# Zero fills of a scratch buffer in an attention and expert kernel: 640 rows an expert from 80 partitions in place of 608 rows from 76

## The chip, the core and the metric

One core of one Trainium2 chip runs the whole program. The metric is the device time of one execution in microseconds (us), lower is better.

## What is computed

Thresholded attention over 4 batches, 8 heads, 576 positions, head size 64; then a layer of 8 experts in which each of the 2304 tokens goes to one expert; then a gated product with two wide matrices. Cut to what matters:

```python
scores = scale * q @ k.T
scores = where(scores >= max(scores) - tau, scores, -1e9)
attn   = softmax(scores)
x      = (attn @ v) as 2304 rows of 512
e      = argmax(x @ w_gate)             # one of 8 experts for each row
x[row] = gate[row] * (relu(x[row] @ w1[e]) @ w2[e])
out    = (x @ w_a) * (x @ w_b) @ w_out
```

## The kernel before, in words

Attention runs head pair by head pair: 16 iterations (4 batches of 4 pairs), each of 9 tiles of scores. For one iteration SyncE (SP) issues the loads of q, k and v (`load`, lines 373, 379 and 381). GpSimd (POOL) splits each into a high and a low part (`split_units`, lines 400 and 414; `raw_k` gives `sk`, `raw_q` gives `sq`, `rv` gives `sv`). TensorE (PE) transposes them (`tq`, line 440), ScalarE (ACT) and VectorE (DVE) write `kT` and `qT`, and SP copies half of `kT` to the other 64 partitions (`swap`, line 446, a transfer of 64 partitions inside the on-chip memory). PE makes the scores (`S_J`, `S_A`, `S_B`, line 654), DVE and ACT the maxima and exponentials, PE transposes the result (line 762), ACT and POOL split it (lines 712 to 727, 803 and 804), SP moves one piece of it across partitions (`tk<-half`, line 783, 64 partitions again), and PE multiplies by v (`pv`, line 838).

After every fourth iteration the rows of a batch are scattered into the scratch buffer `xs` in device memory (helper `scatter`, line 44): one region of 2304 rows for each expert, filled from its start. Later the expert with most rows is read as its first `LEAD` = 256 rows, and the experts as eight items of up to 352 rows, at most 256 rows on. A region can hold fewer tokens than are read, so its first rows are set to zero before the first scatter: 8 experts in `FILLS` = 4 pieces each, 32 transfers (`zero_fill`, line 390). Their source is a tile of zeros in on-chip memory that is read twice by each partition:

```python
n = self.zero_rows // FILLS
self.nc.sync.dma_start(
    self.xs[lo:lo + n].rearrange("(p r) d -> p r d", r=2),
    self.z[0:n // 2].unsqueeze(1).to_broadcast([n // 2, 2, DM]))
```

The order of all work in the attention stage is written out by hand in the string `ORDER` (words `z:0` to `z:31` are the fills, `qe:i:sk0` and `qe:i:sk2` the swaps, `k:i:0` and `k:i:1` the `tk` moves); the fills stand in the first six of the 16 iterations, one to four in a row, between loads, swaps and `tk` moves on SP, which issues them in that order. All of them share one queue, q1. The tile of zeros has the buffer of the scaled rows `xg` of the first batch (tag `xg`, line 1788), so the first write of `xg` (ACT, line 1018) comes after the last fill.

After attention come the experts (from about 420 us) and the gated product (from about 760 us), in which PE multiplies with weights loaded by SP.

Of the kernel before, what the change touches and what calls it, by code (L numbers as in the profile page):

```python
# [31 lines left out]
LEAD = 256  # L32

FILLS = 4
# [1723 lines left out]
@with_exitstack  # L1758
def attention_experts_gated(ctx, tc, q, k, v, tau, w_gate, w1, w2, wa, wb, wo, out):
    nc = tc.nc  # L1760
    NT = q.shape[0] * S
    c = ctx.enter_context(tc.tile_pool(name="consts", bufs=1))
    dp = ctx.enter_context(tc.tile_pool(name="scratch", bufs=1, space=DRAM))
    xs = dp.tile([E * NT, DM], F32, name="xs")
    idt = dp.tile([NT, 1], I32, name="idt")
    idf = c.tile([P, P], F32, name="idf")
    make_identity(nc, idf)
    idr = c.tile([P, P], F32R, name="idr")
    nc.vector.tensor_copy(idr, idf)
    consts = dict(idf=idf, idr=idr)  # L1770
    nb = NT // S
    routing = dict(
        oh=c.tile([P, NB * nb, E], BF16, name="oh"),
        slot=c.tile([P, NB * nb], F32, name="slot"),
        base=c.tile([P, E], F32, name="base"),
        scatters=[],
        lead_relu=[None, None, None],
        lead_high=None,
        sel=c.tile([P, E], F32, name="sel"),
        kept=c.tile([P, 1], F32, name="kept"),  # L1780
        lead=c.tile([P, 1], I32, name="lead"),
        y=[dp.tile([P, 4, LEAD], F32, name=f"lead_y{r}") for r in range(2)],
    )
    routing.update(Experts.constants(nc, c, NT))
    with ExitStack() as ac:
        att = Attention(ac, tc, q, k, v, tau, w_gate, w1, w2, xs, routing, consts)

        att.z = att.xp.tile([P, 4, H, D], F32, tag="xg", name="zero")[:, 0].rearrange("p h d -> p (h d)")
        att.zero_rows = LEAD + max(n for _, n in Experts.ITEMS)
        nc.vector.memset(att.z, 0.0)  # L1790
        att.run()
    ex = Experts(ctx, tc, xs, w1, w2, wa, wb, wo, out, routing, consts, NT)
    ex.order()
    ex.chunk_count()
    ex.experts(idt)
    ex.gated(idt)
# [29 lines left out]
```

## Time and profile before

| what | us |
|---|---|
| median of three runs (1099.53 to 1104.93) | 1100.19 |
| the profiled execution, its own time | 1100.29 |
| its span, first to last instruction | 1098.6 |
| PE busy | 1011.1 (92%) |
| DVE busy | 716.3 (65%) |
| ACT busy | 542.8 (49%) |
| POOL busy | 560.8 (51%) |

Busy time is a sum over a span of stages with different limits; what a stage is limited by is read from the stage's own stretch. A stretch of the trace can be asked for the busy time of each engine, for the granted TensorE clock (1.00 is full), and for the share of 16 DMA engines that were moving packets. A row of the timeline gives the start, the duration, the instruction, and in brackets how long the engine had been idle before and what ended that.

### The profile page before, as it was taken

Reading aid. Unit: us, or ns where it says so; the run is one execution under the profiler, and the core shown is the slowest. Engines: PE = TensorE matmul, PEld = TensorE weight load, DVE = VectorE, ACT = ScalarE, POOL = GpSimd, SP = SyncE. Lnnn points to the kernel's source line nnn. Section 1 sums busy time; section 2 is a strip of 40 time slices with the busy share of each in tenths; the row PEclk is TensorE's granted clock in tenths of the full one; section 3 lists DMA queues with packets and bytes.
Section 4 is the critical chain, followed back from the end, with each engine's and each line's share of the span. In section 5 each row is a group of like instructions: output and inputs, shape, how many; then the busy total and the mean of one; then the engine's idle time right before and its main releaser. Section 6 shows DMA issues by size and latency. Waiting matters only on the chain.

```text
span 1098.6 us, 18663 instructions
## 1 busy us (share of the span) xinstructions
PE 1011.1 (92%) x6392; PEld 918.0 (84%) x6392; DVE 716.3 (65%) x1472; ACT 542.8 (49%) x1118; POOL 560.8 (51%) x515
## 2 busy tenths in 40 slices
PE   3577696999998989999999999999999999999996
PEld 3476696999998989999999998888888888888885
DVE  5655595999999974545568957974592773953213
ACT  4555585999998853545555535321231221321110
POOL 4535566899998764111113426662462653623234
PEclk9978898999999999999999999999999999999999
DMA  5445454545434447665566612340030130200012
GB/s 147 117 125 140 133 134 149 134 114 140 124 78 134 128 137 242 215 193 174 181 188 205 203 48 78 60 75 20 20 78 20 43 73 1 77 20 1 20 58 96
DMA packets 111106, 118.68 MB, mean 108 GB/s; under 512 B 19648, under 2 KB 82112, under 8 KB 111008
## 3 DMA queue, kind: packets, MB, share of 16 engines
q1 hardware_dynamic: 106766, 106.66, 35.0%
q0 software_dynamic: 3840, 10.50, 2.5%
q8 instruction: 51, 0.84, 0.3%
q14 instruction: 47, 0.39, 0.1%
q10 hardware_dynamic: 402, 0.29, 0.1%
HBM read 77.57 MB, written 20.46 MB: 89 GB/s over the span
## 4 chain that ended last, share of the span: by engine, by line
PE 68%; DVE 7%; issue 6%; DMA 6%; POOL 5%; ACT 4%; SPq 3%; POOLq 0%; DVEq 0%; ACTq 0%
PE pg L1709 21%; PE po L1735 10%; PE ph_i L1521 9%; PE py_i L1542 8%; PE pv L838 5%; PE tp L762 3%; PE S_A L654 2%; DMA kT<-kT 2%; PE S_B L654 2%; DMA tk<-half 2%; PE tx L864 2%; PE S_J L654 1%; POOL out L44 1%; SPq L390 1%; DVE mt L667 1%
## 5 line engine op out<-in xcount | busy, mean ns | idle before, releaser
L1709 PE MATMUL pg<-y,w 128*128 128x512 f32 (+1 forms) x1440 | 301.9, 368 | 0.0
L1709 PEld LDWEIGHTS pg<-y,w 128*128 128x128 f32 x1440 | 251.6, 189 | 45.3
L1735 PE MATMUL po<-w,g 128*128 128x512 f32 x648 | 153.3, 390 | 0.6 <-DVE acc L1740 0.6
L1722 POOL TENSOR_TENSOR g<-gg,g 128x512 fp32r<-128x512 f32 (+1 forms) x58 | 76.2, 1313 | 151.1 <-ACT g L1720 151.0
L1735 PEld LDWEIGHTS po<-w,g 128*128 128x128 f32 x648 | 121.0, 188 | 26.1 <-issue 0.8
L727 POOL TENSOR_TENSOR pt<-st,pt 128x512 fp32r<-128x512 f32 x93 | 118.8, 1284 | 18.4 <-ACT pt L717 15.1
L1413 POOL TENSOR_TENSOR w<-raw,w 128x512 fp32r<-128x512 f32 x33 | 45.2, 1372 | 152.1 <-ACT w L1412 152.0
L1521 PE MATMUL ph_i<-xt_i,w 128*128 128x256 f32 (+4 forms) x768 | 117.0, 298 | 3.2 <-DVE w L1413 2.4
L1720 ACT CAST g<-gg 128x512 fp32r<-128x512 f32 (+1 forms) x60 | 34.7, 578 | 169.2 <-PE po L1735 96.2
L1718 DVE TENSOR_TENSOR gg<-ga,pg 128x512 f32<-128x512 f32 (+1 forms) x60 | 37.7, 628 | 122.4 <-PE pg L1709 122.4
L1542 PE MATMUL py_i<-h_i,w 128*128 128x256 f32 (+4 forms) x768 | 112.5, 294 | 0.3 <-PEq L1636 0.3
L838 PE MATMUL pv<-pt,sv 128*128 128x288 f32 x512 | 107.4, 328 | 4.9 <-POOL pt L727 3.6
L1521 PEld LDWEIGHTS ph_i<-xt_i,w 128*128 128x128 f32 x768 | 104.7, 189 | 5.4 <-DVE w L1413 3.6
L1542 PEld LDWEIGHTS py_i<-h_i,w 128*128 128x128 f32 x768 | 104.9, 189 | 0.7 <-issue 0.6
L762 PE MATMUL tp<-idf,P 128*128 128x128 f32 x504 | 94.8, 281 | 3.5 <-DVE P L687 1.6
L1740 DVE TENSOR_TENSOR acc<-acc,po 128x512 f32<-128x512 f32 x108 | 72.7, 683 | 34.3 <-PE po L1735 34.2
L1443 POOL TENSOR_TENSOR t<-t,w 128x512 f32<-128x512 f32 x36 | 53.2, 1477 | 64.0 <-ACT w L1442 47.8
L838 PEld LDWEIGHTS pv<-pt,sv 128*128 128x128 f32 x512 | 77.9, 197 | 6.2 <-POOL pt L727 3.8
L1412 ACT CAST w<-raw 128x512 fp32r<-128x512 f32 x128 | 75.8, 620 | 14.5 <-DMA raw<-in_moe_w 6.9
L1413 DVE TENSOR_TENSOR w<-raw,w 128x512 fp32r<-128x512 f32 x95 | 68.3, 730 | 12.5 <-ACT w L1412 10.6
L762 PEld LDWEIGHTS tp<-idf,P 128*128 128x128 f32 x504 | 64.9, 145 | 5.6 <-DVE P L687 1.9
L1716 ACT COPY ga<-pg 128x512 f32<-128x512 f32 (+1 forms) x60 | 32.6, 544 | 68.6 <-PE pg L1709 68.6
(245 smaller groups left out, 1889.3 us busy)
## 6 DMA issues: line engine op xcount, KB each, us to landing
raw<-in_moe_w SPq DMA_DIRECT2D x128, 256.0 KB
xs<-zero SPq DMA_DIRECT2D x32, 304.0 KB
tk<-half SPq DMA_DIRECT2D x64, 144.0 KB
raw<-in_moe_w_a SPq DMA_DIRECT2D x12, 512.0 KB
raw<-in_moe_w_b SPq DMA_DIRECT2D x12, 512.0 KB
raw<-in_moe_w_out SPq DMA_DIRECT2D x12, 512.0 KB
kT<-kT SPq DMA_DIRECT2D x32, 160.0 KB
kT<-kT SPq DMA_DIRECT2D x32, 144.0 KB
```

Source lines behind the costliest of these rows:

```text
L654: nc.tensor.matmul(ps[:, n, 0:HALF], lhs, kT[:, r, k0 + n * HALF:k0 + (n + 1) * HALF], start=(j == 0), stop=(j == len(seq) - 1),)
L727: nc.gpsimd.tensor_sub(lo, st, fr(hi))
L762: nc.tensor.transpose(st["ps"][:, 128 * j:128 * j + 128], parts(j), idf)
L838: nc.tensor.matmul(R["v", n][:, 0:HALF], lhs, z, start=(c == 0 and r == 0), stop=(c == 4))
L1412: nc.scalar.copy(hi_t, raw)
L1413: engine.tensor_sub(lo_t, raw, fr(hi_t))
L1521: nc.tensor.matmul(ps[:, 0:n], w[a][:, k, :], xt[b][k][:, 0:n], start=(s_ == 0), stop=(s_ == len(steps) - 1))
L1542: nc.tensor.matmul(st["y"][d][:, 0:n], w[a][:, 0, d * P:d * P + P], h[b][:, 0:n], start=(f == 0 and d % each == 0 and (a, b) == (0, 0)), s ...
L1709: mm = nc.tensor.matmul(ps[:, 0:n], w[g][j][m][a][:, k, :], self.y[b][:, k, c0:c0 + n], start=(s_ == 0), stop=(s_ == len(steps) - 1))
L1722: last = low.tensor_sub(gl[:, 0:n], gt[:, 0:n], fr(gh)[:, 0:n])
L1735: nc.tensor.matmul(ps, res[j][a][:, t * P:t * P + P], w[g][j][2][b][:, 0, :], start=(s_ == 0), stop=(s_ == len(steps) - 1))
L1740: nc.vector.tensor_tensor(acc[:, tt, :], acc[:, tt, :], ps, op=ALU.add)
```

## The change

The rows an expert are rounded up to a multiple of 32 times `FILLS`, so that a piece is 160 rows from 80 partitions in place of 152 rows from 76:

```diff
-        att.zero_rows = LEAD + max(n for _, n in Experts.ITEMS)
+        att.zero_rows = -(-(LEAD + max(n for _, n in Experts.ITEMS)) // (32 * FILLS)) * 32 * FILLS
```

The 32 transfers stand at the same places of the same queue, each of 320 KB in place of 304 KB; every engine has the same instructions in the same order as before. No other transfer changes.

## Rows read from the trace of the kernel before

**Rows 1.** The page's 40 equal slices of the span (27.5 us each), busy tenths and clock.

```profile
PE   3577696999998989999999999999999999999996
...
PEclk9978898999999999999999999999999999999999
```

**Rows 2.** The fills' instructions on SP: duration in ns least, median, most; first and last start.

```profile
L390 SPq DMA_DIRECT2D xs<-zero x32: 684/744/4216, 17.9 to 170.4; - x32
```

**Rows 3.** Busy time by stretch: us, engines, clock, DMA share of 16 engines, GB/s.

```profile
20.00:40.00 20.00, 14.02 (x97) 12.10 (x96) 17.32 (x39) 15.63 (x30) 12.27 (x13) 1.00 0.42 124
40.00:190.00 150.00, 104.89 (x736) 100.29 (x736) 87.98 (x220) 89.94 (x190) 83.60 (x85) 0.84 0.50 135
190.00:350.00 160.00, 156.25 (x1268) 149.33 (x1266) 150.05 (x378) 150.46 (x321) 145.35 (x147) 1.00 0.43 116
```

**Rows 4.** Waits of PE from 40 to 190 us: in total, times, longest.

```profile
PE pv L838 <- DMA tk<-half: 26.7, 4, 10.9
PE S_J L654 <- DMA kT<-kT: 9.2, 2, 6.2
PE pv L838 <- POOL pt L727: 3.6, 1, 3.6
PE S_B L654 <- DVE P L687: 3.3, 2, 3.1
PE pv L838 <- POOL pt L804: 0.8, 1, 0.8
```

**Rows 5.** Timeline of SP, issues of loads among the fills and after them.

```profile
33.67 1.61 SPq L373 DMA_DIRECT2D raw_k<-in_k  x1
...
36.87 4.00 SPq L373 DMA_DIRECT2D raw_q<-in_q  x1
...
207.68 0.47 SPq L373 DMA_DIRECT2D raw_q<-in_q  x1
```

**Rows 6.** Timeline of POOL, splits that wait for loads.

```profile
46.63 0.67 POOL L400 TENSOR_SCALAR sk<-raw_k 128x576 fp32r<-128x576 f32 x1 [7.26 <-DMA raw_k<-in_k]
...
168.44 0.72 POOL L400 TENSOR_SCALAR sv<-rv 128x640 fp32r<-128x640 f32 x1 [6.87 <-DMA rv<-in_v]
```

**Rows 7.** Timeline of ACT, the first write of `xg`.

```profile
181.87 0.72 ACT L1018 ACTIVATE xg<-x,g 128x512 f32<-128x512 f32 x1 [3.07 <-DMA xs<-zero]
```

**Rows 8.** Timeline of DVE, what waited for ACT's next exponential.

```profile
183.25 0.82 DVE L687 SCALAR_TENSOR_TENSOR P<-S_B,m_B,e_B 128x576 f32<-128x576 f32 x1 [3.11 <-ACT e_B L675]
```

**Rows 9.** Waits of PE from 190 to 350 us.

```profile
PE pv L838 <- DMA tk<-half: 0.4, 1, 0.4
```

**Rows 10.** DMA from 168 to 176 us: packets by size; the queue's packets, MB, share of 16 engines.

```profile
DMA packets 374, 0.74 MB, mean 93 GB/s; under 512 B 13, under 2 KB 13, under 8 KB 374
...
q1 hardware_dynamic: 374, 0.74, 26.0%
```

**Rows 11.** DMA from 17.9 to 176 us, from the first fill on: the same queue.

```profile
q1 hardware_dynamic: 15249, 20.40, 47.3%
```

**Rows 12.** DMA from 176 to 178 us, when swaps of `kT` are under way: the queue.

```profile
q1 hardware_dynamic: 195, 0.39, 84.8%
```

**Rows 13.** Timeline of PE, score products after a wait and without one.

```profile
133.81 1.78 PE L654 MATMUL S_J<-kT,qj 128*128 128x288 f32 x6 [6.25 <-DMA kT<-kT]
...
205.67 1.30 PE L654 MATMUL S_J<-kT,qj 128*128 128x288 f32 x8
```

**Rows 14.** DMA from 1060 to 1098.6 us, when `out` is written: GB/s in 40 slices, the queue.

```profile
GB/s 127 144 17 259 13 0 0 0 0 0 0 8 0 0 98 174 272 170 102 0 272 0 0 0 0 0 246 106 191 225 144 174 0 272 191 81 0 8 0 0
...
q0 software_dynamic: 970, 3.15, 21.4%
```

## The prediction

> **What bounds the kernel now.** First the page's slices [rows 1]: from the eighth slice on (about 190 us) PE is busy nine tenths nearly throughout, but before that it stands between 3 and 7 tenths in all slices but one, and the granted clock dips below full in most of them. The kernel is bound by PE except in its first 190 us, and the 32 fills are issued from 17.9 to 170.4 us [rows 2], inside that part.
>
> Second, the stretches [rows 3]. From 190 to 350 us the same attention work runs with no fill: 1268 matmuls in 160 us, PE idle for 3.75 us, clock 1.00. From 40 to 190 us only 736 matmuls are done in 150 us: PE is idle for 150 − 104.89 = 45.1 us and the mean clock is 0.84. At the later pace (160 / 1268 = 0.1262 us a matmul) 736 take 92.9 us, so this stretch loses **57.1 us**. DVE, ACT and POOL are no busier there than 60%, so none of them is the limit. From 20 to 40 us PE also has gaps, but I leave that stretch out: it is the first iteration, with DVE busy 17.3 of 20 us.
>
> Third, what ends PE's waits from 40 to 190 us [rows 4]. DMA ends 26.7 us (`tk`) and 9.2 us (`kT`) directly. 3.6 us come through POOL: its split of `raw_k` started at 46.6 us after a wait of 7.3 us for a load issued at 33.7 us, 13 us earlier [rows 5, 6]. 0.8 us comes through POOL's wait of 6.9 us for `rv` [rows 6]. And 3.1 of the 3.3 us behind DVE come from the first write of `xg`, in whose buffer the zeros lie: ACT waited 3.07 us there for the fills, its next exponential was late, and DVE waited 3.11 us for that [rows 7, 8]. Together 26.7 + 9.2 + 3.6 + 0.8 + 3.1 = **43.4 us** of the 45.1 us end in a transfer. From 190 to 350 us PE waits 0.4 us for `tk` and for no other DMA [rows 9]: the moves are the same, the fills are gone.
>
> Fourth, why the transfers are late. From 168 to 176 us the queue moves almost nothing but fills: 361 of 374 packets are 2 KB or more, and the share is 26.0% of 16 engines, which is 4.2 engines, at 93 GB/s [rows 10]. I read this as a fill from 76 partitions lying on **four of the 16 DMA engines**. A packet then takes 0.26 x 16 x 8 us / 374 = 89 ns. One fill is 152 rows of 2 KB: 13.5 us of engine time, 3.4 us on four engines. 32 fills are 433 us, or 108 us on each of the four. All of the queue from 17.9 to 176 us is 47.3% of 16 engines for 158.1 us, 1197 us [rows 11]. The 764 us that are not fills, spread evenly, make 48 us on each engine. So four engines have 108 + 48 = 156 us of work in 158 us and are full, and the other twelve have 48. A transfer spread over all engines lands when its slowest part does, so each `kT`, `tk` and load waits behind the fills on those four. The queue also pushes back on SP: issuing a `raw_q` load took 4.00 us at 36.9 us and 0.47 us at 207.7 us [rows 5].
>
> **The change part by part.**
>
> *More bytes.* 8 more rows a fill, 32 times: 256 packets of 89 ns, 23 us of engine time, 1.4 us on each of 16 engines. SP issues the same 32 transfers at a median of 744 ns [rows 2] in the same order. Cost on the path: nothing, as long as the engines aren't full; if they stayed on four, 23 / 4 = 5.7 us.
>
> *Spread.* No row shows 80 partitions. The nearest are the swaps, of 64: from 176 to 178 us, right after the fills drained, swaps of `kT` alone hold 84.8% of 16 engines, that is 13.6 or more [rows 12]. So it isn't a small number of partitions that confines a transfer; 64 divides evenly among 16 engines and 76 doesn't, and 80 does, by five each. Bounds: four engines as now (no gain) and 16. I take 16, as nearest to the swaps. A fill is then 160 x 89 / 16 = 0.89 us on each engine in place of 3.4 us on four, against 0.74 us to issue it: a run of four fills leaves well under a microsecond of backlog in place of some ten. Work for each engine: 32 x 0.89 + 48 = 76 us, where four had 156.
>
> The Trainium skill ("DMA: Bandwidth & Descriptors", Why a DMA increments its semaphore by 16 and not by 1) says that a transfer gets the largest number up to 16 that divides the slowest dimension on both sides, which makes 4 of 76 and 16 of 80; no row shows the second. The same page (Specifications) gives 8 partitions an engine as a convention, which would put 76 and 80 both on ten engines and leave the time where it is; the 26.0% above, 4.2 engines rather than ten, speak against it.
>
> *Waits that go.* The 43.4 us above, if each transfer lands as it does after 190 us. *The clock.* After each long wait PE runs at the lower of its two levels for a while: six `S_J` products took 1.78 us after a wait of 6.25 us, and eight took 1.30 us with no wait [rows 13]. Over the stretch 736 matmuls took 104.89 us where the later mean (156.25 / 1268 = 123 ns) makes 90.7 us: 14.2 us more, and these go with the waits. Sum: 43.4 + 14.2 = 57.6 us, the same as the 57.1 us from the pace, which I take as the ceiling since the later stretch is bound by PE.
>
> *What is late next.* Not all of it comes back. The 764 us of other traffic and the fills' 456 us must now fit in some 110 us of 16 engines, a share near 0.7, where the undisturbed stretch has 0.43 [rows 3]. `tk` is the one move that was late there at all [rows 9], so it has no slack, and behind a run of fills it will be late again by one or two microseconds. Six or so such places with a short dip of the clock: I leave **10 us** in, an estimate between 0 and half of the 57. After 190 us PE is busy throughout, so what comes earlier there brings the end forward by as much.
>
> Gain: 57 − 10 = 47 us. The profiled execution took 1100.29 us, a span of 1098.6 and 1.7 around it, 0.1 us from the median of the runs: 1100.3 − 47 = **1053 us**.
>
> **The rivals.**
>
> *A half gain.* The fills, now on all 16 engines in runs of up to four, still hold up every `tk` and swap behind them, and PE falls back to the lower clock each time. For it: the share of 0.7. Against: nothing was late at 0.43, and the fills drain about as fast as SP issues them. A third to a half of the 57 us comes back: 1072 to 1081 us.
>
> *Nothing changes.* The fills stay on few engines, or the four full engines weren't what the moves waited for. For it: no row shows 80 partitions. Against: the four-engine share stands at 26% while the swaps reach 85%. Time 1100 us, at most 1106 with the added bytes.
>
> *Slower, by the far end of the fills.* If 93 GB/s [rows 10] is what device memory takes in from this pattern rather than what four engines give, a fill of 320 KB holds all 16 queues for 3.5 us in place of four. Other transfers end with their slowest part, so they gain nothing, and the fills' added 5% (0.18 us each) come on top: 32 x 0.18 = 5.7 us, 1106 us. It decides from the point at which a fill takes over 3.4 us to drain. Against: at the end the writes of `out`, into the same memory, reach 272 GB/s in a slice, and 3.15 MB take 21.4% of 16 engines for 38.6 us, 24 GB/s an engine [rows 14], the same as 93 / 4 = 23. The rate follows the engines.
>
> **How the numbers follow.** A measurement of this kernel tells a difference of about 0.5% (5.5 us) from none. The forecast, 35 to 59 us faster, has 0.76; a half or third of the gain 0.17; nothing 0.04; slower 0.03. So faster 0.93, same 0.04, slower 0.03. The low end is the whole 57 us and two for what 20 to 40 us may give: 1041. The high end takes in most of the half gain, 20 us: 1080. What lies outside is the weaker end of the half gain and the two last cases, near 0.15.
>
> **What would show it.** Right: no stretch with a DMA share flat near 0.26 before 190 us; a fill's packets draining near 0.9 us; raw loads issued in about half a microsecond; PE's waits for `tk` and `kT` down from 36 us to under 10, the clock near 1.00 from 50 us on; the matmuls that ended at 190 us now ending near 143 us, and every later stage as long as before. Wrong: fills still at 26% (the spread); spread fills but `tk` waits of several microseconds each (the 10 us); or a gain before 190 us that is given back in the experts' weights.

## The result, and the profile after

| | us |
|---|---|
| before, median of four runs (1099.53 to 1104.93) | 1100.36 |
| changed, median of four runs (1043.88 to 1050.26) | 1049.39 |
| changed, the profiled execution, its own time | 1050.08 |
| its span | 1048.4 |

The ratio is 0.9518, with a 95% interval of 0.9476 to 0.956: 51 us faster, 4 us more than forecast and inside the range.

The page's slices after (26.2 us each), against [rows 1]:

```profile
PE   3899999999989899999999999999999999999996
...
PEclk9999999999989999999999999999999999999999
DMA  5877645436343486655666223510220310300012
```

From the third slice on PE is at nine tenths, but for two slices at eight; it used to be there from the eighth slice on. The busy time by stretch, with the columns of [rows 3]:

```profile
20.00:40.00 20.00, 14.04 (x95) 12.13 (x95) 17.12 (x39) 15.37 (x30) 12.67 (x14) 1.00 0.72 199
40.00:143.00 103.00, 100.94 (x815) 96.74 (x815) 96.34 (x243) 97.58 (x208) 89.55 (x92) 1.00 0.70 196
143.00:190.00 47.00, 45.37 (x365) 43.12 (x364) 42.12 (x103) 42.65 (x92) 43.29 (x44) 1.00 0.44 120
190.00:350.00 160.00, 154.22 (x1218) 147.65 (x1216) 145.03 (x364) 140.44 (x296) 134.89 (x136) 0.98 0.44 121
```

The stretch in which the fills lie now runs at the pace of the stretch without them: 103 / 815 = 0.1264 us a matmul, against 0.1262 after 190 us before the change. The clock is 1.00 in it, and the DMA share is 0.70, as worked out. From 20 to 40 us PE's busy time did not change.

All waits of PE from 40 to 143 us that the view lists, where five rows of up to 26.7 us stood [rows 4]:

```profile
PE tp L762 <- ACT pt L717: 0.5, 1, 0.5
PE tp L762 <- ACT qT L458: 0.4, 1, 0.4
PE S_B L654 <- DVE P L687: 0.4, 2, 0.3
PE tp L762 <- DVE x L872: 0.4, 1, 0.4
PE pv L838 <- ACT o L843: 0.2, 1, 0.2
```

No DMA is among them. The fills' instructions on SP [rows 2], and a `raw_q` load issued behind three fills [rows 5], after:

```profile
L390 SPq DMA_DIRECT2D xs<-zero x32: 605/628/1814, 18.1 to 119.0; - x32
```

```profile
33.83 0.49 SPq L373 DMA_DIRECT2D raw_q<-in_q  x1
```

The queue pushes back far less: 0.49 us for the issue that took 4.00 us, though the `raw_k` load just ahead of it still took 1.23 us (1.61 before).

On how many engines a fill from 80 partitions lies is read from 118 to 123 us, while the last four fills drain. SP issued them from 116.87 to 120.22 us:

```profile
116.87 3.35 SPq L390 DMA_DIRECT2D xs<-zero  x4
```

```profile
DMA packets 715, 1.33 MB, mean 267 GB/s; under 512 B 70, under 2 KB 70, under 8 KB 714
...
q1 hardware_dynamic: 714, 1.32, 93.2%
```

93.2% is 14.9 engines, so these fills lie on all 16. A packet takes 0.932 x 16 x 5 / 714 = 104 ns, a little more than the 89 ns before. 320 KB at 267 GB/s are 1.2 us a fill, and the fills drain until about 123 us (from 123 to 124 us the share is 9.9%), nearly 3 us after the last was issued.

**Where the gain ends up.** Taking the same instruction in both traces shows how far it has moved. Two issues of SP before, in order of time, and the same two after:

```profile
206.66 0.37 SPq L373 DMA_DIRECT2D raw_k<-in_k  x1
...
950.96 0.37 SPq L1432 DMA_DIRECT2D raw<-in_moe_w_b  x1
```

```profile
150.26 0.37 SPq L373 DMA_DIRECT2D raw_k<-in_k  x1
...
900.76 0.37 SPq L1432 DMA_DIRECT2D raw<-in_moe_w_b  x1
```

Right behind the fills the program is 206.66 − 150.26 = 56.4 us ahead, in the gated product (whose first product, L1709, starts at 644 us before, not at about 760) only 950.96 − 900.76 = 50.2 us. So between these two executions 6.2 us were given back on the way, in places that have no fill. Two of them show in PE's timeline, before:

```profile
351.49 1.11 PE L864 MATMUL tx<-W,o 128*128 128x72 f32 x8 [2.64 <-DVE half L721]
...
627.09 1.46 PE L1521 MATMUL ph_i<-xt_i,w 128*128 128x256 f32 x10 [1.92 <-DVE w L1413]
```

and after, the same products behind the same waits:

```profile
296.31 1.99 PE L864 MATMUL tx<-W,o 128*128 128x72 f32 x8 [2.65 <-DVE half L721]
...
575.37 2.31 PE L1521 MATMUL ph_i<-xt_i,w 128*128 128x256 f32 x10 [1.92 <-DVE w L1413]
```

PE waited equally long in both kernels. Before, it came back at the higher of its two levels (the granted clock was 1.00 from 351 to 355 us), after, at the lower one (0.50 from 296 to 300 us). Whether this belongs to the change is asked in the last run.

### The profile page after: what moved, and what is told of

It reads as the page before. It is cut to its first block, busy times and chain, and to the rows that moved or that the text cites. A ratio compares the mean times of both kernels' runs of the same rounds, so it can differ in the third digit from the quotient of the medians.

```text
span 1048.4 us, 18663 instructions
## 1 busy us (share of the span) xinstructions
PE 1002.2 (96%) x6392; PEld 909.6 (87%) x6392; DVE 715.5 (68%) x1472; ACT 541.0 (52%) x1118; POOL 560.8 (53%) x515
## 4 chain that ended last, share of the span: by engine, by line
PE 51%; issue 5%; POOL 3%; DVE 3%; ACT 1%; DMA 0%; POOLq 0%; SPq 0%; DVEq 0%; ACTq 0%
PE pg L1709 22%; PE po L1735 10%; PE ph_i L1521 9%; PE py_i L1542 9%; POOL out L44 1%; PE px_i L1496 1%; POOL w L1444 1%; POOL t L1443 1%; DVE w L1413 1%; DVE acc L1740 1%; DVE a L1435 1%; POOL g L1722 0%; DMA raw<-in_moe_w 0%; DVE t L1439 0%; DVE u L1436 0%
## 5 line engine op out<-in xcount | busy, mean ns | idle before, releaser
L1709 PE MATMUL pg<-y,w 128*128 128x512 f32 (+1 forms) x1440 | 301.9, 368 | 0.0
L1709 PEld LDWEIGHTS pg<-y,w 128*128 128x128 f32 x1440 | 251.6, 188 | 45.3
L1735 PEld LDWEIGHTS po<-w,g 128*128 128x128 f32 x648 | 120.9, 188 | 26.2 <-issue 0.8
L838 PE MATMUL pv<-pt,sv 128*128 128x288 f32 x512 | 103.3, 320 | 0.2 <-ACT o L843 0.2
L762 PE MATMUL tp<-idf,P 128*128 128x128 f32 x504 | 91.9, 274 | 3.7 <-DVE P L687 1.6
L838 PEld LDWEIGHTS pv<-pt,sv 128*128 128x128 f32 x512 | 74.9, 190 | 0.9 <-ACT o L843 0.5
L1526 DVE SCALAR_TENSOR_TENSOR h_i<-ph_i,h_i 128x256 fp32r<-128x256 f32 (+4 forms) x64 | 28.9, 451 | 60.5 <-ACT h_i L1525 60.5
L1525 ACT ACTIVATE h_i<-ph_i 128x256 fp32r<-128x256 f32 (+4 forms) x64 | 26.0, 407 | 84.4 <-PE ph_i L1521 63.7
```

The costliest lines, as they stand in the source:

```text
L762: nc.tensor.transpose(st["ps"][:, 128 * j:128 * j + 128], parts(j), idf)
L838: nc.tensor.matmul(R["v", n][:, 0:HALF], lhs, z, start=(c == 0 and r == 0), stop=(c == 4))
L1709: mm = nc.tensor.matmul(ps[:, 0:n], w[g][j][m][a][:, k, :], self.y[b][:, k, c0:c0 + n], start=(s_ == 0), stop=(s_ == len(steps) - 1))
L1735: nc.tensor.matmul(ps, res[j][a][:, t * P:t * P + P], w[g][j][2][b][:, 0, :], start=(s_ == 0), stop=(s_ == len(steps) - 1))
```

## The experiments

The theory to be tested: a fill lies on a number of DMA engines that its partitions set, the full engines make every other transfer late, and it is the spread alone, not the 32 rows more, that gave the 51 us. The rivals: the round number of rows; a fixed number of partitions for an engine; a queue's order in place of full engines. Each run has the kernel before beside it on the same chip, with medians of 1099.8 to 1100.5 us. The 106 us that the expectations name is the changed kernel's stretch from 18 to 124 us, the counterpart of 17.9 to 176 us before [rows 11].

### 608 rows, all spread

```diff
-        n = self.zero_rows // FILLS
-        lo = e * self.NT + part * n
+        n = (160, 160, 160, 128)[part]
+        lo = e * self.NT + part * 160
```

> 608 rows an expert as before, but in pieces of 160, 160, 160 and 128 rows from 80, 80, 80 and 64 partitions. Theory (a transfer lies on the largest number of engines up to 16 that divides its partitions evenly, and four engines were full): all pieces lie on 16 engines, each engine has 433 / 16 + 48 = 75 us of work, so the time is that of the change, 1047 to 1051 us, and no stretch shows a DMA share near 0.26. Rival (the number of rows matters, 640 being a round number): 608 rows stay at 1100 us.

Measured: 1048.17 us, ratio 0.9534 (0.9507 to 0.9561), the time of the change. Of the two things that the change does, rows and partitions, only the partitions count. The rival is out.

### 77 partitions

```diff
+        att.zero_rows = 154 * FILLS
```

> 616 rows an expert, 154 from 77 partitions. Theory: 77 divides evenly by 11, so 11 engines with 32 x 154 x 0.089 / 11 + 48 = 88 us of work, below the 106 us that the first part takes in the changed kernel: 1047 to 1055 us. Rival (rows, or that only a multiple of 16 partitions helps): near 1100 us.

Measured: 1048.61 us, ratio 0.9543 (0.9516 to 0.9569). One partition more than before, and the whole gain is there. Where fills run nearly alone (119.5 to 122 us) the queue shows

```profile
q1 hardware_dynamic: 243, 0.45, 61.2%
```

which is 9.8 of the eleven engines of the theory. It need not be 16. An issue of a fill took SP 910 ns here (the median), where the change has 628, and that cost nothing.

### 85 partitions

```diff
+        att.zero_rows = 170 * FILLS
```

> 680 rows an expert, 170 from 85 partitions: more rows and more partitions than the change. Theory: 85 divides evenly by 5, so five engines with 32 x 170 x 0.089 / 5 + 48 = 145 us of work, 39 us over the 106 us of the changed kernel's first part: about 1088 us (1078 to 1098), and a DMA share near 5 / 16 = 0.31 where the fills run alone. Rivals (rows; or eight partitions to an engine, which gives 85 partitions 11 engines): 1050 to 1054 us.

Measured: 1102.85 us, ratio 1.0027 (1.001 to 1.0043). More partitions than in the change, and none of the gain, which puts both rivals out. Where a fill runs alone (168 to 172 us) the queue shows

```profile
q1 hardware_dynamic: 226, 0.45, 32.0%
```

which is 5.1 of 16 engines, the five of the theory. But the time is a miss: 1088 us was expected. Worked out with this run's own packets (0.32 x 16 x 4 / 226 = 91 ns), each of the five engines has 147 us of work, 9 us less than the four engines of before, and the time shows none of it: PE still waits 24.6 us for `tk` and 10.0 us for `kT` from 40 to 190 us. The sum of an engine's work tells full from not full; among kernels whose engines are nearly full it was not good to 15 us.

### 82 partitions

```diff
+        att.zero_rows = 164 * FILLS
```

> 656 rows an expert, 164 from 82 partitions. Theory: 82 divides evenly by 2, so two engines with 32 x 164 x 0.089 / 2 + 48 = 282 us of work, 176 us over 106: about 1225 us (1180 to 1260), slower than the kernel before, with a DMA share near 2 / 16 = 0.125 where the fills run alone. Rivals (rows; or eight partitions to an engine): 1050 to 1054 us.

Measured: 1198.07 us, ratio 1.0906 (1.0867 to 1.0944). Two partitions more than in the change cost 149 us. From 80 to 96 us, fills alone:

```profile
q1 hardware_dynamic: 393, 0.79, 13.0%
```

13.0% is 2.1 engines at 50 GB/s. Two, four, five engines show 50, 93 and 112 GB/s: the rate goes with the number of engines, at 22 to 25 GB/s each, so it isn't the far end that limits a fill on so few engines. On 16 it is 267 GB/s, as shown above for the changed kernel, 17 to 18 an engine: there the rate no longer goes with the number alone, but it is almost three times the 93.

### 8 partitions of 19 rows

```diff
-            self.xs[lo:lo + n].rearrange("(p r) d -> p r d", r=2),
-            self.z[0:n // 2].unsqueeze(1).to_broadcast([n // 2, 2, DM]),
+            self.xs[lo:lo + n].rearrange("(p r) d -> p r d", p=8),
+            self.z[0:8].unsqueeze(1).to_broadcast([8, n // 8, DM]),
```

> 608 rows in pieces of 152 as before, but each from 8 partitions of 19 rows in place of 76 of 2: the same bytes, rows and order, far fewer partitions. Theory (engines by even division): eight engines with 433 / 8 + 48 = 102 us of work, just under the 106 us of the changed kernel's first part: 1047 to 1065 us, a DMA share up to 0.5 where fills run alone. Rival (many partitions make a fill fast, or eight partitions make one engine): 8 partitions are slower than 76, well over 1100 us.

Measured: 1174.62 us, ratio 1.0673 (1.0639 to 1.0708): far slower, as the rival said. From 104 to 112 us, fills alone, packets by size and the queue:

```profile
DMA packets 209, 0.41 MB, mean 51 GB/s; under 512 B 9, under 2 KB 9, under 8 KB 209
...
q1 hardware_dynamic: 209, 0.41, 45.8%
```

45.8% is 7.3 engines, so about the eight that the theory gave are at work, but a packet takes 0.458 x 16 x 8 / 209 = 281 ns in place of 89. The number of engines isn't the only thing that sets the drain of a fill. Each engine here reads 19 times from one partition, at 51 / 8 = 6.4 GB/s; before, each of the four read from 19 partitions, at 23 GB/s.

### 16 partitions of 10 rows

```diff
-            self.xs[lo:lo + n].rearrange("(p r) d -> p r d", r=2),
-            self.z[0:n // 2].unsqueeze(1).to_broadcast([n // 2, 2, DM]),
+            self.xs[lo:lo + n].rearrange("(p r) d -> p r d", p=16),
+            self.z[0:16].unsqueeze(1).to_broadcast([16, n // 16, DM]),
```

> The changed kernel's 640 rows in pieces of 160, each from 16 partitions of 10 rows in place of 80 of 2: 16 engines either way. In the run with 8 partitions of 19 rows the share was 0.46 but the rate 51 GB/s, 281 ns a packet in place of 89. Theory P (one partition gives out some 6.4 GB/s, 51 / 8, to repeated reads): 16 partitions give 102 GB/s, a fill takes 3.2 us, the rings have 32 x 3.2 + 48 = 150 us of work: 1085 to 1110 us, a share near 1 at 100 GB/s where fills run alone. Theory B (the eight partitions share one way out, of 51 GB/s, and so do these 16): 6.4 us a fill, 253 us of work, over 1170 us. Theory E (only the number of engines matters, and the run with 8 partitions was slow for having eight): 1047 to 1051 us.

Measured: 1091.78 us, ratio 0.9917 (0.9882 to 0.9952). From 158 to 168 us:

```profile
DMA packets 550, 1.02 MB, mean 102 GB/s; under 512 B 51, under 2 KB 51, under 8 KB 550
...
q1 hardware_dynamic: 550, 1.02, 91.3%
```

Nearly all 16 engines are busy and move 102 GB/s, 6.4 from each partition. Theory P's numbers hold, and the other two fall as they were put: twice the partitions, twice the rate, and 16 engines are little help when a fill is read from 16 partitions (1091.78 us against 1049.39 from 80). So a fast fill needs both: a count that divides among many engines, and many partitions to read from. Where the limit lies is not shown. It may be the single partition, an engine that reads only one partition, the reading of one row 19 or 10 times over, or a way out that a few neighbouring partitions share: 51 and 102 GB/s are as well 25.5 for every four partitions. All of these give the same two rates, and no run here takes them apart.

### 81 partitions

```diff
+        att.zero_rows = 162 * FILLS
```

> 648 rows an expert, 162 from 81 partitions. Theory (engines by even division): nine engines with 32 x 162 x 0.089 / 9 + 48 = 99 us of work, under the 106 us of the changed kernel's first part, but close: 1048 to 1065 us, a DMA share near 9 / 16 = 0.56 where the fills run alone. Rival (after the runs with 85 partitions and with 8: only 16 engines or nearly as many help, whatever the sum of the work says): over 1085 us.

Measured: 1058.51 us, ratio 0.9622 (0.9584 to 0.9661), most of the gain. Where fills run nearly alone (60 to 62.5 us) the queue shows 52.7% of 16, 8.4 of the nine engines of the theory:

```profile
q1 hardware_dynamic: 209, 0.41, 52.7%
```

The rival is out. With 99 us of work in 106 the moves are late by a little: PE waits 4.1 us for `tk` and 2.5 us for `kT` from 20 to 190 us.

### Each fill twice

```diff
-        self.nc.sync.dma_start(
+        for lo in (lo, lo + self.zero_rows): self.nc.sync.dma_start(
```

> The changed kernel with each fill issued twice, the second for 160 rows that nothing reads: 64 transfers from 80 partitions. It doubles what the fills still cost. Theory (on 16 engines they cost nothing while the engines aren't full): each engine has 2 x 28.5 + 48 = 105 us of work, as much as the 106 us that PE needs, so the engines are at their limit: SP issues 20 us more, the `tk` and `kT` moves are late by a few us, 1055 to 1080 us. Rival (the fills still hold up the moves in the changed kernel, a cost that doubles with them): PE's waits for DMA were near 0 before 143 us, so there is nothing to double and this rival also needs the limit; it would give 1049 to 1052 us only if the fills are free altogether.

Measured: 1074.83 us, ratio to before 0.9763 (0.9733 to 0.9792), 25 us over the change. PE's waits from 40 to 190 us:

```profile
PE pv L838 <- DMA tk<-half: 13.6, 3, 7.0
PE S_B L654 <- DVE P L687: 4.4, 4, 3.8
PE S_J L654 <- DMA kT<-kT: 4.4, 1, 4.4
```

The fills of the change cost nothing that shows, and as many again cost 25 us: the limit lies between. The engines are closer to full, with a DMA share of 0.86 from 40 to 143 us where the change has 0.70, but SP has more to do as well:

```profile
40.00:143.00 103.00, 84.96 (x643) 82.33 (x642) 75.51 (x180) 75.94 (x159) 69.93 (x70) 0.90 0.86 241
```

```profile
L390 SPq DMA_DIRECT2D xs<-zero x64: 604/758/1715, 17.7 to 148.0; - x64
```

64 issues at 758 ns are 49 us of SP's time, where 32 at 628 ns were 20, and the moves stand behind them in SP's order. This run does not tell full engines from a later issue.

### The fills in a queue of their own

```diff
-        self.nc.sync.dma_start(
+        self.nc.scalar.dma_start(
```

> The kernel before (608 rows, 76 partitions) with the 32 fills issued by ScalarE in place of SyncE, at the same places of the order, so that they lie in a queue of their own. Theory A (the four engines are full, so whatever shares them is late): the fills take 108 us on four engines as before; the moves may pass some of them, but the first write of the scaled rows waits for the last fill, and ScalarE is held up while it issues: 1085 to 1115 us. Theory B (the moves were late because they stood behind fills in the same queue): they pass the fills now, 1050 to 1070 us.

Measured: 1113.16 us, ratio 1.0127 (1.0089 to 1.0164): 1.3% slower than before. Waits of PE from 40 to 190 us, and of ACT:

```profile
PE tp L762 <- ACT js L806: 15.9, 1, 15.9
PE S_J L654 <- DMA kT<-kT: 7.5, 1, 7.5
...
PE pv L838 <- DMA tk<-half: 2.5, 2, 1.9
```

```profile
ACT js L806 <- DMA xs<-zero: 10.3, 1, 10.3
```

The issue of three fills by ACT just ahead of that wait, and the fills' own queue from 64 to 71 us:

```profile
62.72 8.57 ACTq L390 DMA_DIRECT2D xs<-zero  x3
```

```profile
q10 hardware_dynamic: 301, 0.60, 22.0%
```

Half of each theory seems to hold. PE waits 10.0 us for `tk` and `kT` in place of 35.9 [rows 4], as it would if the moves passed many of the fills in another queue; but PE is also held up by ACT now, which may hide waits for the moves, so how much of their lateness was standing behind fills is not shown. The fills are still on few engines (22.0% is 3.5), and now the queue pushes back on ACT, which PE then waits for: 8.57 us for the issue of three fills. The total falls to theory A.

### The change once more

No edit.

> The changed kernel again, nothing altered, for the two places after 190 us at which its profile lost what the kernel before did not: the products after a wait of 2.65 us for `half` (1.99 us in place of 1.11) and after a wait of 1.92 us for `w` (2.31 us in place of 1.46). Theory (the clock falls or not after the same wait, by chance from run to run): the two products take another time in this profile, and the runs spread over some 6 us, 1043 to 1051. Rival (the change itself moved something there): 1.99 and 2.31 us again, and no run under 1047 us.

Measured: 1048.06 us, six runs from 1045.37 to 1050.06, ratio 0.9518 (0.9494 to 0.9542). The two places in its profile:

```profile
296.16 1.11 PE L864 MATMUL tx<-W,o 128*128 128x72 f32 x8 [2.64 <-DVE half L721]
...
573.53 1.89 PE L1521 MATMUL ph_i<-xt_i,w 128*128 128x256 f32 x10 [1.92 <-DVE w L1413]
```

The first group takes 1.11 us again and the second 1.89, but the clock fell at both places here too, only later (at the second it was 0.58 from 574 to 576 us). At the first:

```profile
298.00:300.00 2.00, 2.00 (x12) 1.98 (x11) 1.48 (x3) 1.95 (x4) 1.69 (x2) 0.50 0.88 240
```

So the two values alone do not clear the change. Other kernels do. The 85-partition kernel, which has none of the gain, took 1.98 and 1.64 us at the two places; the 77-partition and the 608-row kernel, which have all of it, took 1.46 and 1.45 us at the second. And the whole stretch between the two issues of SP used above, from `raw_k` to `raw` in the gated product, took 744.3 us in the kernel before and 750.5 in the changed one, but 746.4 to 748.8 in the ten other traces, this one (748.8) and kernels with no gain among them (85 partitions 747.3, 16 of 10 rows 748.2). The two executions that were compared happened to be the shortest and the longest of twelve. Even the wait of 1.10 us for `tk` at 161.9 us, behind the fills, which comes again in this second trace (1.06 us) and which the kernel before lacks, is found in kernels with no gain (1.00 us with 82 partitions) and is missing in kernels with all of it (608 rows, 77 partitions). So none of the 6.2 us is shown to belong to the change; it fits the spread of the runs.

### All kernels side by side

Work is that of one engine that carries fills, by the prediction's sum (48 us of other traffic, and the fills at the packet time or, for the two of few partitions, the measured 51 and 102 GB/s).

| fills | engines | work, us | median, us |
|---|---|---|---|
| 82 x 2 rows | 2 | 282 | 1198.07 |
| 8 x 19 rows | 8 | 243 | 1174.62 |
| 76 x 2 rows (before) | 4 | 156 | 1100.36 |
| 16 x 10 rows | 16 | 151 | 1091.78 |
| 85 x 2 rows | 5 | 145 | 1102.85 |
| 80 x 2 rows, each twice | 16 | 105 | 1074.83 |
| 81 x 2 rows | 9 | 99 | 1058.51 |
| 77 x 2 rows | 11 | 88 | 1048.61 |
| 80 x 2 rows (the change) | 16 | 76 | 1049.39 |
| 608 rows, 80 and 64 x 2 | 16 | 75 | 1048.17 |

Below some 90 us of work the fills are hidden behind PE; from there on the time rises with the work on the whole, though not in order among the three of 145 to 156 us. No version is faster than the change by more than the runs spread.

## Why the prediction was right

*Four engines.* Shown. The flat share of 0.26 is gone, and other numbers of partitions put the share where even division puts it or a little below: 13.0% for two engines, 32.0% for five, 52.7% for nine, 61.2% for eleven, 93.2% for the 16 of the change. The Trainium skill ("DMA: Bandwidth & Descriptors", Why a DMA increments its semaphore by 16 and not by 1) gives this rule (the largest number up to 16 that divides both sides), and the runs agree with it in every case, 80 partitions included. The convention of eight partitions an engine, which the Trainium skill gives on the same page (Specifications), would have put 77, 82 and 85 alike on ten or eleven engines, and they lie 150 us apart.

*More bytes cost nothing.* Right: 608 and 640 rows, spread alike, take 1048.2 and 1049.4 us.

*The waits, 43.4 us, and the clock, 14.2 us.* Right together: in the two traces the program is 56.4 us ahead after the fills, against the 57.1 us that the pace gave as the ceiling. PE's 815 matmuls took 100.94 us, 124 ns each, where 123 were expected.

*What is late next, 10 us.* This is the term that was mis-sized. Nothing was late while the fills ran: PE had no wait for a transfer from 40 to 143 us, although the share was 0.70. Not that nothing was left to wait for: a fill drained in 1.2 us, not in 0.89, so four in a row left nearly 3 us of backlog where well under a microsecond was forecast. But no wait of PE fell on it; behind the last four fills SP issued its next swap at 123.41 us, after they had drained. From 143 to 350 us PE waits 1.6 us for `tk`. The doubled fills show that the room was small: there the waits for `tk` and `kT` are 18 us.

*What comes earlier before 190 us brings the end forward by as much.* Between the two profiled executions this failed by 6.2 us, and it covered the 10 us that were too many: 57 − 10 = 47 was forecast, 56.4 − 6.2 = 50.2 came. Part of the 6.2 us went to the clock after waits that both kernels have, and the twelve traces fit the spread of executions. That the forecast lay within 4 us is therefore partly luck: two errors of opposite sign. The medians give 51 and, in the change's second set of runs, 52 us; whether the rest of the 57 us is lost after the fills, or the one trace of the kernel before had a longer first part than most, is open.

*The half gain* would have needed moves late by several microseconds at a share of 0.7; they weren't. *Slower by the far end* is out, by the rates at two, four and five engines and by the 267 GB/s at 16. That a fill's own source could be a limit was in neither the sum nor the rivals; the change didn't touch it, with five partitions to an engine. The chances leave 0.07 for the two last cases and little of the 0.17 beyond 1080 us, which is less than the 0.15 that was put outside the range; nothing else rests on it.

## What to carry to other kernels

A DMA share that stands flat at k/16 while one shape of transfer runs alone (here 13%, 26% and 32% for two, four and five) suggests that this shape lies on k engines. Those k can be full while the mean share is a half (0.50 here), and transfers spread over all 16 are then late. Look at the number of partitions of each transfer and choose one that divides among many engines (80 did, and so did 77), even if it takes a few more bytes (5% here cost nothing), but keep a source of many partitions. Price a spread transfer by the work that it leaves on the busiest engine, and compare that with the time that the bounding engine needs in the same stretch.

## What was not expected

- Fills read from 8 and from 16 partitions ran at 51 and 102 GB/s with most of the engines that they lay on busy, 6.4 GB/s for each partition, and a packet of 2 KB took 281 ns in place of 89.
- After the same wait of 1.92 us PE stayed at the higher level in some executions (1.46 us for ten products) and fell to the lower in others (1.89 and 2.31 us in the changed kernel's two). Runs of the changed kernel differ by some 6 us (1043.88 to 1050.26), and the stretch without fills by as much between traces (744.3 to 750.5). What decides it is open.
- Why five engines with 147 us of work were no faster than four with 156 is open too. SP took longer to issue a fill from 85 partitions (a median of 884 ns against 744), some 4.5 us over 32 fills; that this is the reason was not tried, and the 77-partition kernel took 910 ns an issue at no cost, though its engines had more room (88 us of work in 106).
